# Recurrent attention over 64 segments on one core: every second step runs its projections in reverse, the last projection's streamed weights stay for the next step, nine stream slots

## The chip, the cores and the metric

One core of one Trainium2 chip runs one program. The metric is the device time in microseconds. TensorE (PE), VectorE (DVE), ScalarE (ACT), GpSimd (POOL) and SyncE (SP, which here only issues loads) work side by side and wait for one another by semaphores; 16 DMA engines move data between HBM and the on-chip memory.

## The reference

```python
# A: x (1, 2048, 1024) layer-normed, 64 segments of 32 rows; 32 heads of 128; 8 memory rows
mem = mem0
for s in range(n_seg):                       # 64 steps, each needs the last one's output
    h = concatenate([mem, xs], axis=1)       # 8 + 32 rows
    q, k, v = h @ Wq, h @ Wk, h @ Wv         # 1024 -> 4096 each
    p = softmax(where(mask, q @ k.T * scale, -1e9))
    o = (p @ v) @ Wo                         # 4096 -> 1024
    mem = o[:, :M, :]                        # the next step's memory rows
    outs.append(o[:, M:, :])
# B: the two rows with the largest x @ w_r pass through a gated MLP (1024 -> 3584 -> 1024)
# result: x + A + B
```

The four weight matrices together are 32 MB in bf16, more than fits on chip; all of them are needed in each of the 64 steps, which follow one another.

## The kernel before

The weights are cut in 64 **granules** of 128x2048 (512 KB). Granules 0 to 47 belong to Q, K and V: eight granules per half matrix (16 heads), numbered q0, k0, q1, k1, v0, v1 (0/1 is the half); 48 to 63 are the output projection, two heads each. A step goes through seven **passes** p: 0 to 5 are the six half projections in that order, 6 is the output projection of 16 granules; (p, kc) is a place in them.

Forty-four granules are resident on chip. Twenty are streamed (`STREAMED`): loaded anew in every step by SP, in the order of their use, into five rotating slots. `fetch` issues the next load as soon as `after` reports a slot's granule as used up. Two exceptions keep weights in PSUM: granule 6 (`KEPT_WHOLE`) is not loaded at all, `bring_back` copies its four pieces from PSUM; of granule 25 (`KEPT_PART`) only half is loaded and `kept_piece` copies the rest. In step 0 everything comes from the inputs; `keep` turns the kept pieces into PSUM, and `copy_block` writes each other streamed granule to a DRAM scratch `wsc`, contiguous, which all later steps load from.

Each granule is multiplied with the step's 32 rows (`ST`; 24 rows of the segment and 8 memory rows) in four matmuls of 512 columns on four column strips of PE. The last eight rows of each of the four segments of a group do not depend on the memory, so their projections are made once per group of four steps, spread as extra passes over the granules (`PASSES`, the "left-over rows", tiles `PSl`, `WL`); their Q and K go through DRAM (`ql_d`) and come back as `LX`.

What follows a projection is hung up at fixed places by `hook(p, kc, ...)`, run after that granule's matmuls: `transposes` turns q and k, `scores` multiplies them, adds the mask on DVE, takes the maximum and subtracts it, `exponent` is on ACT, `soften` normalises and transposes the probabilities to `PT` on DVE, `attend` multiplies them with V (two halves `ph` per half of the heads) and casts the sums to `OT`. Half 0's scores stand at (2, 6) and its attention at (5, 4) and (5, 6); half 1's scores at (4, 6), exponent at (5, 0), attention in the output projection ahead of its granules 5 and 8. In that projection the next segment is normalised and turned too. A step ends with the DVE addition of the output (line 842), the stores, and the turning of the new memory rows into the next `ST`.

Lines in the profile: 354 the streamed load in `fetch`, 388 `copy_block`, 365 and 370 the turnings in `keep`, 377 `bring_back`, 381 `kept_piece`, 774 the projections' matmuls (`PSm`), 567 the left-over passes, 574 `project` (`WO` for the step, `WL` for left-over rows), 624 `transposes`, 490 the turning of `LX` (fetched in 483), 647 and 649 `scores`, 656 to 662 mask, maximum and subtraction, 666 `exponent`, 671 to 682 `soften`, 696 and 698 `attend`, 705 and 707 its casts, 793 and 803 the casts of a finished projection, 842 the step's last addition. The changed kernel has its own numbers.

After the last step the MoE weights are loaded into the homes of the residents and the two routed rows are done.

```python
def fetch():
    s, g = flow.pop(0)
    t = wstream.tile([P, 2048], BF16, tag="g", name="g")
    ...
        nc.sync.dma_start(out=t[:, c], in_=wsc[g][:, :])
# (5, 6): attend(0, 1); output projection:
for w in range(16):
    if w == 5:
        attend(1, 0)
    if w == 8 and s + 1 < NSEG:
        attend(1, 1, lambda: turned.append(turn_rows(xn, left_too)))
    Gv = granule(48 + w)
    project(WO, w, Gv, lhs_main, w == 15, first=(w == 0))
```

Of the kernel before, what the change touches and what calls it, by code (L numbers as in the profile page):

```python
# [17 lines left out]
N_RES = 44  # L18
N_SLOT = 5
KEPT_WHOLE = 6  # L20
KEPT_PART = 25
NEG = -30000.0

PHASES = [(0, 0), (1, 0), (0, 1), (1, 1), (2, 0), (2, 1)]

STREAMED = [2, 5, 6, 9, 13, 17, 21, 25, 29, 33, 36, 39, 42, 45, 47, 50, 53, 56, 59, 62]

UNIT_PHASE = {"q0": 0, "k0": 1, "q1": 2, "k1": 3, "v0": 4, "v1": 5, "o": 6}
PASSES = {
# [11 lines left out]
}  # L44

COPIES = {"q0": (1, 1, 0, "scalar"), "q1": (1, 5, 7, "vector"), "k0": (2, 2, 0, "scalar"), "k1": (3, 1, 0, "scalar"),
          "v0": (3, 4, 7, "scalar"), "v1": (3, 5, 7, "scalar"), "o": (0, 4, 3, "vector")}
# [3 lines left out]
def kernel(  # L51
# [46 lines left out]
    assert len(streamed) == NG - N_RES  # L98
    n_str = len(streamed)
    resident = [g for g in range(NG) if g not in streamed]  # L100

    def granule_dram(g):
        if g < 48:
            p, kc = divmod(g, KC)
            mat, half = PHASES[p]
# [11 lines left out]
    wstream = ctx.enter_context(tc.tile_pool(name="wstream", bufs=N_SLOT))  # L117
# [24 lines left out]

    def load_resident(g):
# [11 lines left out]
    NEGR = CT[:, 13:14]  # L155
# [8 lines left out]
    PTB2 = BT[:, 256:512].bitcast(BF16)  # L164
    OPB = BT[:, 256:256 + 4 * NK]
# [110 lines left out]
    def norm_seg(s):  # L276

        x = X[s % 2]
        mr = two_rows(MR[:, s, :], "ri")
        ab = mr[:, 2:4]  # L280
        nc.vector.tensor_scalar(out=ab[:, 0:1], in0=mr[:, 1:2], scalar1=1.0, scalar2=KMSK, op0=ALU.add, op1=ALU.mult)
        nc.vector.tensor_scalar(out=ab[:, 1:2], in0=mr[:, 0:1], scalar1=mr[:, 1:2], scalar2=-1.0, op0=ALU.mult, op1=ALU.mult)
        xn = front.tile([P, 256], BF16, tag="st", name="XN")
        nc.vector.tensor_scalar(out=xn[:, :], in0=x[:, :], scalar1=mr[:, 0:1], scalar2=mr[:, 1:2],
                                op0=ALU.subtract, op1=ALU.mult)
        nc.vector.tensor_scalar(out=x[:, :], in0=x[:, :], scalar1=ab[:, 0:1], scalar2=ab[:, 1:2],
                                op0=ALU.mult, op1=ALU.add)
        return xn

    def turn(src, at=0):  # L290
        PTx = PTB[:, 256 * at:256 * (at + 1)].rearrange("p (c g r) -> p c g r", c=2, g=4)
# [8 lines left out]
    def turn_rows(xn, xl):  # L300

        return turn(xn), turn(xl, 1) if xl is not None else None

    def new_st(turned):
        PTx, PTl = turned
        st = front.tile([P, KC, SEG], BF16, tag="st", name="ST")
        nc.scalar.copy(out=gview(st)[:, :, :, 0:XM], in_=PTx[:, :, :, 0:XM])
        if PTl is None:
            return st, None
        stl = one.tile([P, KC, SEG], BF16, tag="stl", name="STL")  # L310
        nc.scalar.copy(out=gview(stl), in_=PTl[:, :, :, :])
        return st, stl
# [16 lines left out]
    def sum_left(t, G):  # L329
# [9 lines left out]
    queued = []  # L339
# [3 lines left out]
                 KEPT_PART: {2: KEPT[2][:, 0:512], 3: KEPT[2][:, 512:1024]}}  # L343

    def fetch():
        if not flow:
            return
        s, g = flow.pop(0)
        t = wstream.tile([P, 2048], BF16, tag="g", name="g")
        c = columns(g, s)  # L350
        if s == 0:
            nc.sync.dma_start(out=granule_out(t, g), in_=granule_dram(g))
        elif c is not None:
            nc.sync.dma_start(out=t[:, c], in_=wsc[g][:, :])
        queued.append((g, t))
# [4 lines left out]

    def keep(g, t):
        for c, K in KEPT_COLS[g].items():
            turned = PTB.rearrange("p (i r) -> p i r", i=4)
            for i in range(4):
                nc.tensor.transpose(out=turned[:, i, :], in_=t[:, 512 * c + P * i:512 * c + P * (i + 1)],
                                    identity=IDENT[:, :])
            XK = one.tile([P, 512], BF16, tag="vl0", name="XK")
            nc.vector.tensor_copy(out=XK[:, :], in_=PTB)
# [4 lines left out]
    back = [None] * 4  # L373

    def bring_back(c, copy):
        back[c] = one.tile([P, 512], BF16, tag=(roles[0], "bE", "kt", "bC")[c], name="BK")
        copy(out=back[c][:, :], in_=KEPT_COLS[KEPT_WHOLE][c])  # L377

    def kept_piece(g, c, copy):
        t = [t for q, t in queued if q == g][0]  # L380
        copy(out=t[:, 512 * c:512 * (c + 1)], in_=KEPT_COLS[g][c])  # L381


# [6 lines left out]
    to_copy = list(streamed)  # L390
    flow += [(s, g) for s in range(NSEG) for g in streamed if s == 0 or g != KEPT_WHOLE]

# [5 lines left out]
    def fetch_moe():  # L398
        while moe and free_homes:
            what = moe.pop(0)  # L400
            h = free_homes.pop(0)
            t = home(h, [P, 2048], BF16, "MW") if h >= 0 else wstream.tile([P, 2048], BF16, tag="g", name="g")
# [9 lines left out]
    def granule(g):  # L412
        if g in res_tiles:
            return res_tiles[g]
        got, t = queued.pop(0)
        assert got == g, (got, g)
        return t
# [11 lines left out]
    n_q = 0  # L429
    for g in range(48):  # L430
        if g in streamed:
            n_q += 1
            if n_q < N_SLOT:
                fetch()
            continue
        if n_q >= N_SLOT:
            break
        load_resident(g)
        if g % 2 == 1 and n_x < NT // 2:
            load_x(n_x)  # L440
            n_x += 1
    todo_res = [g for g in resident if g not in res_tiles]
# [4 lines left out]
    ST, STL = new_st(turn_rows(norm_seg(0), XL0))  # L447
# [11 lines left out]
    def after(s, g):  # L459

        if s == 0:
            if g in side:
                side[g]()
            if g % 2 == 1 and g >= 8 and to_copy:
                copy_block(to_copy.pop(0))
            if n_x_left and g % 2 == 1:
                load_x(n_x_left.pop(0))
            while todo_res and todo_res[0] <= g + 2 * 64 // n_str + 8 and (todo_res[0] < resident[-10] or g >= 2 * NT + 12):
                load_resident(todo_res.pop(0))
        if g in streamed and (s == 0 or g != KEPT_WHOLE):  # L470
            fetch()
        if s == NSEG - 1:
            if g in resident:
                free_homes.append(g)
            if not flow:
                fetch_moe()
# [493 lines left out]
```

## Time and profile before

| | |
|---|---|
| median of 3 runs | 1895.43 us (1892.03 to 1902.41) |
| profiled execution | 1896.06 us, of it span 1894.4 us |
| busy share | PE 83%, DVE 46%, ACT 36%, POOL 23% |
| DMA | 712.41 MB, mean 376 GB/s |
| TensorE clock granted | mean 0.960 |

"Busy" is the share of the span in which an engine had an instruction running; for PE the ends of matmuls are modelled, so busy isn't full speed. In the digits of the slices, 9 is 90% or more. In rows of waits the numbers are the total in us, how often, and the longest. In timeline rows they are start, duration, engine, line, operation, output and inputs.

### The profile page before, as it was taken

To read this page: it belongs to the slowest core of one execution; us is meant where nothing else is said; L and a number is where in the kernel's file an instruction comes from. 1 tells how busy PE (TensorE), PEld (TensorE's weight loads), DVE (VectorE), ACT (ScalarE), POOL (GpSimd) and SP (SyncE) were. 2 spreads that over 40 slices of the span, in tenths; PEclk is the share of its full clock that TensorE was granted. 3 is DMA by queue.
4 is the path that set the end of the run, shared out by engine and by line. 5 is a ranking of instruction groups with operands and counts; after the bars stand their busy time and mean duration, and the time that the engine had idled before them with its cause. 6 is when DMAs were issued, how large, how long until landed. Compare 5 with 4: busy or idle time off the path is not lost.

```text
span 1894.4 us, 82425 instructions
## 1 busy us (share of the span) xinstructions
PE 1572.3 (83%) x36000; PEld 880.0 (46%) x36000; DVE 875.6 (46%) x2865; ACT 683.5 (36%) x1916; POOL 441.5 (23%) x882
## 2 busy tenths in 40 slices
PE   3458888889888888898888988888888889888864
PEld 1124545455454444445454545445444554545443
DVE  6734544445444444544454444444444454444430
ACT  1123433344333433434333334333433343433320
POOL 3111313213131322213121322213132221312120
PEclk8669999999999999999999999999999999999985
DMA  9999999999999999999999999999999999999998
GB/s 370 398 368 379 369 386 373 391 378 390 393 360 375 368 380 372 379 372 374 401 365 374 370 388 370 355 383 374 379 364 387 377 392 378 364 395 362 374 388 331
DMA packets 232121, 712.41 MB, mean 376 GB/s; under 512 B 39296, under 2 KB 53168, under 8 KB 231760
## 3 DMA queue, kind: packets, MB, share of 16 engines
q1 hardware_dynamic: 194384, 671.18, 92.9%
q0 software_dynamic: 28736, 28.09, 4.6%
q10 hardware_dynamic: 8640, 7.87, 1.2%
q8 instruction: 282, 4.62, 0.9%
q14 instruction: 79, 0.65, 0.1%
HBM read 694.32 MB, written 22.29 MB: 378 GB/s over the span
## 4 chain that ended last, share of the span: by engine, by line
DMA 53%; PE 38%; DVE 5%; issue 2%; ACT 1%; SPq 1%; ACTq 0%; DVEq 0%
DMA g<-wsc 47%; PE PSm L774 21%; PE WO L574 4%; PE PSl L567 4%; PE BT L624 3%; PE WL L574 2%; DMA XP<-in_A_x_dram 2%; DMA MW<-in_B_w_gate_dram 1%; DVE XR L248 1%; DMA MW<-in_B_w_up_dram 1%; DMA g<-in_A_Wq_dram 1%; DMA wres<-in_A_Wo_dram 1%; PE BS L647 1%; DMA g<-in_A_Wo_dram 1%; PE BT L293 1%
## 5 line engine op out<-in xcount | busy, mean ns | idle before, releaser
L774 PE MATMUL PSm<-wres,ST 128*32 128x512 bf16 x8448 | 706.5, 383 | 9.1 <-DMA wres<-in_A_Wv_dram 3.5
L774 PEld LDWEIGHTS <-ST 128*32 128x32 bf16 x12288 | 328.6, 96 | 403.5 <-issue 176.3
L774 PE MATMUL PSm<-g,ST 128*32 128x512 bf16 x3588 | 361.9, 387 | 106.2 <-DMA g<-wsc 81.5
L574 PEld LDWEIGHTS <-OT 128*32 128x32 bf16 x8192 | 219.2, 97 | 153.3 <-issue 135.8
L793 ACT CAST XB<-PSm 128x512 bf16<-128x512 f32 x256 | 150.1, 586 | 310.8 <-PE PSm L774 309.9
L574 PE MATMUL WO<-wres,OT 128*32 128x256 bf16 x5632 | 238.3, 278 | 13.7 <-DMA wres<-in_A_Wo_dram 7.9
L483 POOL DMA_DIRECT2D LX<-ql_d x63 | 33.6, 533 | 825.9 <-PE WO L574 396.5
L574 PE MATMUL WO<-g,OT 128*32 128x256 bf16 x2560 | 132.3, 281 | 83.6 <-DMA g<-wsc 74.1
L567 PE MATMUL PSl<-wres,STL 128*32 128x512 bf16 x2112 | 192.7, 391 | 0.0
L844 POOL DMA_DIRECT2D out_dram<-X x256 | 129.4, 512 | 217.1 <-DVE X L842 168.3
L639 DVE COPY KT<-BT 128x512 bf16<-128x512 bf16 x112 | 45.7, 408 | 283.3 <-ACT XB L793 119.0
L273 POOL DMA_DIRECT2D X<-in_A_x_dram x256 | 129.7, 510 | 186.4 <-PE PSm L774 83.8
L377 ACT COPY BK<-KEPT 128x512 bf16<-128x512 bf16 x126 | 74.4, 590 | 129.3 <-PE WO L574 98.3
L632 ACT COPY QT<-BT 128x512 bf16<-128x512 bf16 x128 | 74.9, 585 | 122.2 <-PE BT L490 70.3
L567 PEld LDWEIGHTS <-STL 128*32 128x32 bf16 x3072 | 83.6, 98 | 54.0 <-issue 8.4
L624 PEld LDWEIGHTS <-XB 128*128 128x128 bf16 x1024 | 58.5, 98 | 107.6 <-ACT XB L793 66.4
L842 DVE TENSOR_TENSOR X<-WO,X 128x256 bf16<-128x256 f32 x64 | 27.2, 424 | 170.9 <-PE WO L574 170.9
L803 ACT CAST VM<-PSm 128x512 bf16<-128x512 f32 x128 | 75.6, 591 | 81.2 <-PE PSm L774 79.6
L696 PEld LDWEIGHTS <-VM 32*128 32x128 bf16 x2048 | 66.1, 91 | 82.9 <-issue 69.9
L624 PE MATMUL BT<-IDENT,XB 128*128 128x128 bf16 x1024 | 102.0, 222 | 1.4 <-ACT QKL L502 1.4
L381 DVE COPY g<-KEPT 128x512 bf16<-128x512 bf16 x126 | 47.6, 419 | 118.2 <-PE PSm L774 74.4
L705 DVE CAST OT<-BT 128x128 bf16<-128x128 f32 x128 | 37.3, 291 | 129.8 <-PE BT L293 68.8
(168 smaller groups left out, 2378.9 us busy)
## 6 DMA issues: line engine op xcount, KB each, us to landing
g<-wsc SPq DMA_DIRECT2D x1134, 512.0 KB, 6.1
g<-wsc SPq DMA_DIRECT2D x63, 256.0 KB, 5.4
LX<-ql_d POOLq DMA_DIRECT2D x63, 128.0 KB, 5.9
ql_d<-XBl ACTq DMA_DIRECT2D x60, 128.0 KB, 5.6
MW<-in_B_w_gate_dram SPq DMA_DIRECT2D x16, 448.0 KB, 9.1
MW<-in_B_w_up_dram SPq DMA_DIRECT2D x16, 448.0 KB, 9.1
wres<-in_A_Wk_dram SPq DMA_DIRECT2D x12, 512.0 KB, 11.5
MW<-in_B_w_down_dram SPq DMA_DIRECT2D x12, 512.0 KB, 10.1
```

The source lines that it names most:

```text
L273: nc.gpsimd.dma_start(out=X[s % 2][32 * g:32 * g + XM, :], in_=x2[s * SEG:s * SEG + XM, 256 * g:256 * (g + 1)])
L377: copy(out=back[c][:, :], in_=KEPT_COLS[KEPT_WHOLE][c])
L381: copy(out=t[:, 512 * c:512 * (c + 1)], in_=KEPT_COLS[g][c])
L567: nc.tensor.matmul(PSl[32 * jq:32 * jq + 32, :], lhsT=STL[:, g % KC, :], rhs=part(Gv, jq), start=first_, stop=last_, tile_position=(0, 32 ...
L574: nc.tensor.matmul(PS[32 * g:32 * g + 32, 0:256], lhsT=lhs(h), rhs=Gv[:, D * hs + 256 * g:D * hs + 256 * (g + 1)], start=(first and hs == ...
L624: nc.tensor.transpose(out=PTq[:, il, :, :].rearrange("p j r -> p (j r)"), in_=XB[:, il * P:(il + 1) * P], identity=IDENT[:, :])
L632: nc.scalar.copy(out=QT[half][:, :, :], in_=pv)
L696: nc.tensor.matmul(o, lhsT=VM[half][q0:q0 + 32, il * P:(il + 1) * P], rhs=PTm[q0:q0 + 32, il, 0:NK], start=True, stop=False, tile_position ...
L774: nc.tensor.matmul(PSm[32 * jq:32 * jq + 32, :], lhsT=ST[:, kc, :], rhs=part(Gv, jq), start=(kc == 0), stop=(kc == KC - 1), tile_position= ...
L793: nc.scalar.copy(out=XB[:, :], in_=PSm[:, :])
L803: nc.scalar.copy(out=VM[half][:, :], in_=PSm[:, :])
L844: nc.gpsimd.dma_start(out=out2[s * SEG:s * SEG + XM, 256 * g:256 * (g + 1)], in_=OB[32 * g:32 * g + XM, :])
```

## The change

- Even steps run v0, q0, k0, q1, k1, v1; odd steps v1, q1, k1, q0, k0, v0 (`ORDER`; `a` is the half that comes first, `b` the other). So the pass before the output projection and the next step's first pass use the same eight granules. Five of them are streamed, and they are not loaded for the next step: they stay in their slots (`held_over`) until its first pass has used them. Within the output projection odd steps begin with granules 56 to 62.
- Nine slots in place of five; 39 residents and three quarters of granule 12 (`PIECED`) in place of 44; the fourth quarter of 12 is kept in PSUM. Streamed: 24. `KEPT_WHOLE` is now granule 63, the last of the step; `bring_back` copies it at places 9 and 11 of the output projection.
- Scores, exponent and attention have new places: half a's scores at (3, 6), attention at (5, 3) and (5, 6); half b's scores at (5, 5), exponent and `soften` at (5, 6) behind the second attention of a, attention in the output projection ahead of place 7 (even) or 6 (odd), and 9.
- The mask is put into the scores' PSUM by three PE matmuls with the identity ahead of the scores; DVE no longer adds it. `norm_seg` is split, and part of it stands earlier. `LX` is fetched behind place 15 of the output projection, before behind 9, and turned in pass 2, before in pass 1. Some copies change between ACT and DVE. `PASSES` and `COPIES` are new throughout (one entry shown).

```diff
-N_RES = 44
-N_SLOT = 5
-KEPT_WHOLE = 6
+N_SLOT = 9
+KEPT_WHOLE = 63
 KEPT_PART = 25
+PIECED = 12
-STREAMED = [2, 5, 6, 9, 13, 17, 21, 25, 29, 33, 36, 39, 42, 45, 47, 50, 53, 56, 59, 62]
+STREAMED = [1, 5, 9, 13, 17, 21, 25, 27, 30, 35, 36, 37, 38, 39, 43, 44, 45, 46, 47, 50, 53, 58, 61, 63]
+V_FIRST, V_LAST = [3, 4, 5, 6, 0, 1, 7, 2], [3, 0, 1, 4, 5, 6, 7, 2]
+O_ORDER = [list(range(48, 64)), [*range(56, 63), *range(48, 56), 63]]
+def order_of(odd):
+    a, b = odd, 1 - odd
+    out = [[32 + 8 * a + c for c in V_FIRST]]
+    out += [[16 * half + 8 * mat + c for c in range(8)] for half in (a, b) for mat in range(2)]
+    return out + [[32 + 8 * b + c for c in V_LAST], O_ORDER[odd]]
-    "v1": {(3, 5, 2): [42], (3, 5, 3): [40, 41], (3, 5, 4): [43], ...
+    "v1": {(2, 6, 5): [40], (2, 6, 6): [41], (2, 7, 0): [42, 43], ...
...
+    def held_over(s, g):
+        return s + 1 < NSEG and g in ORDER[s % 2][5] and g in streamed
+    def loaded(s, g):
+        return g in streamed and (s == 0 or not (g == KEPT_WHOLE or g in ORDER[s % 2][0]))
...
     def fetch():
-        s, g = flow.pop(0)
-        t = wstream.tile([P, 2048], BF16, tag="g", name="g")
+        while flow and slots:
+            s, g = flow.pop(0)
+            slot = slots.pop(0)
+            t = wres.tile([P, 2048], BF16, tag=slot, name="g")
...
-        if g in streamed and (s == 0 or g != KEPT_WHOLE):
+        if g in queued and not held_over(s, g):
+            slots.append(queued.pop(g)[0])
             fetch()
...
+            if mat == 1:
+                for S4, m in ((SPS[:, :, 0, 0:XM], MASK), (SPS[:, :, 0, SEG:NK], NEGR.to_broadcast([P, XL])),
+                              (SPS[:, :, 1, SEG:NK], MASK[:, 0:XL])):
+                    nc.tensor.matmul(S4, lhsT=IDENT[:, :], rhs=m.unsqueeze(1).to_broadcast([P, 4, S4.shape[2]]),
+                                     start=(m is MASK), stop=False, skip_group_check=True)
...
-        hook(2, 6, lambda: scores(0))
-        hook(3, 4, exponent)
-        hook(3, 4, lambda: soften(0))
+        hook(3, 6, lambda: scores(a))
+        hook(4, 1, exponent)
+        hook(4, 1, lambda: soften(a))
...
-        hook(4, 6, lambda: scores(1))
-        hook(5, 0, exponent)
-        hook(5, 0, lambda: soften(1))
-        hook(5, 4, lambda: attend(0, 0))
-        hook(5, 6, lambda: attend(0, 1))
+        hook(5, 3, lambda: attend(a, 0))
+        hook(5, 5, lambda: scores(b))
+        hook(5, 6, lambda: attend(a, 1))
+        hook(5, 6, exponent)
+        hook(5, 6, lambda: soften(b))
...
+        for n, g in enumerate(order[6]):
+            if n == 7 - a:
+                attend(b, 0)
+            if n == 9 and s + 1 < NSEG:
+                attend(b, 1, lambda: turned.append(turn(xn, BS[:, 160:288].bitcast(BF16))))
...
+            if s > 0 and n in (9, 11):
+                c = n // 2 - 4
+                bring_back(c, a, nc.vector.tensor_copy)
+                bring_back(2 + c, a, nc.scalar.copy)
```

More of the change, by code (lines that the diff above doesn't have):

```diff
@@ L412, in granule @@
     def granule(g):
[L413 to L417, printed above, removed]
+        if g == PIECED:
+            return list(pieced)
+        if g == KEPT_WHOLE and g not in queued:
+            return back
+        return res_tiles[g] if g in res_tiles else queued[g][1]
     load_x(0)
@@ L446 @@
     norm_left(XL0, 0)
-    ST, STL = new_st(turn_rows(norm_seg(0), XL0))
+    MR0 = norm_rows(0)
+    ST = new_st(turn(norm_seg(0, MR0), PTS[:, 0:256]))
+    sum_seg(0, MR0)
+    STL = new_stl(turn(XL0))
     mem_to_st(OB, ST)
@@ L473, in after @@
             if g in resident:
-                free_homes.append(g)
+                free_homes.append(f"wres{g}")
             if not flow:
+                free_homes.extend(slots)
+                slots.clear()
                 fetch_moe()
@@ L770 @@
             for kc in range(KC):
-                g = 8 * p + kc
-                Gv = back if s > 0 and g == KEPT_WHOLE else granule(g)
+                g = order[p][kc]
+                Gv = granule(g)
                 for jq in range(4):
-                    nc.tensor.matmul(PSm[32 * jq:32 * jq + 32, :], lhsT=ST[:, kc, :], rhs=part(Gv, jq),
+                    nc.tensor.matmul(PSm[32 * jq:32 * jq + 32, :], lhsT=ST[:, g % KC, :], rhs=part(Gv, jq),
                                      start=(kc == 0), stop=(kc == KC - 1), tile_position=(0, 32 * jq))
```

329 lines of the change are left out of this document (181 added, 148 removed), and 22 rows, old and new, of the table PASSES.

## The prediction

> **What bounds the kernel now.** I read the page first, then the DMA queues over the steady part, then the steps and waits there, then single timelines. A "step" is one of the 64 segments; a "granule" is one 128x2048 piece of weight (512 KB); "position" is a granule's place in its step, 0 to 63, with 48 to 63 the output projection; even and odd are the step's number.
>
> ```profile
> span 1894.4 us, 82425 instructions
> PE 1572.3 (83%) x36000; PEld 880.0 (46%) x36000; DVE 875.6 (46%) x2865; ACT 683.5 (36%) x1916; POOL 441.5 (23%) x882
> DMA  9999999999999999999999999999999999999998
> DMA 53%; PE 38%; DVE 5%; issue 2%; ACT 1%; SPq 1%; ACTq 0%; DVEq 0%
> ```
>
> PE is busy 83% of the time and the DMA line never leaves its top digit, so the question is which of the two gives the other its pace. The chain that ended last is more DMA than PE. The next rows are the DMA queues from 130 to 1838 us, the busy times of the same stretch, and the one DVE addition (line 842) that closes each of the 64 steps.
>
> ```profile
> DMA packets 206514, 642.51 MB, mean 376 GB/s; under 512 B 36191, under 2 KB 49871, under 8 KB 206171
> q1 hardware_dynamic: 172795, 612.27, 94.1%
> 130.00:1838.00 1708.00, 1496.98 (x34690) 838.11 (x34689) 791.82 (x2645) 661.35 (x1866) 406.38 (x805) 0.99 1.00 376
> L842 DVE TENSOR_TENSOR X<-WO,X x64: 423/425/426, 129.4 to 1837.7; 128x256 bf16<-128x256 f32 x64
> ```
>
> Sixty-three steps lie between 129.4 and 1837.7: **27.12 us a step**. DMA share is 1.00 over all of it: the 16 engines have no free time left, at 376 GB/s. Queue q1, which carries the streamed weights, holds 94.1% of it, 0.941 x 1708 / 63 = 25.51 us a step. A step streams 18 whole granules and one half (1134 and 63 issues over 63 steps on the page), 18.5 in all, so **one granule costs 1.38 us** of DMA time. The page's rows of those issues, the waits of PE in the same stretch, and three granules of one projection as PE takes them:
>
> ```profile
> g<-wsc SPq DMA_DIRECT2D x1134, 512.0 KB, 6.1
> g<-wsc SPq DMA_DIRECT2D x63, 256.0 KB, 5.4
> ...
> PE PSm L774 <- DMA g<-wsc: 81.5, 173, 1.7
> PE WO L574 <- DMA g<-wsc: 74.1, 161, 1.9
> PE WO L696 <- ACT OTL L707: 11.5, 15, 2.1
> ...
> 919.36 0.39 PE L567 MATMUL PSl<-wres,STL 128*32 128x512 bf16 x4
> 919.58 0.39 PE L774 MATMUL PSm<-wres,ST 128*32 128x512 bf16 x4
> 919.79 0.39 PE L774 MATMUL PSm<-g,ST 128*32 128x512 bf16 x4
> ```
>
> 155.6 us, or 2.47 a step, is waiting for streamed weights, in 334 waits; the next kind is 11.5 us. So without DMA waits PE would need at most 27.12 - 2.47 = 24.65 us a step. It may need less: four matmuls are drawn 0.39 us long but follow the last four after 0.22, so each wait can hide some 0.17 us behind matmuls still drawn, 334 x 0.17 / 63 = 0.9 us a step, which gives 23.75 as the lower end.
>
> **The change part by part: traffic.** On SP, between an output projection and the first projections behind it, before (the number after wsc is the granule, the one behind it the buffer):
>
> ```order
> L354 DMA g_21274<-wsc62_123 128x2048
> L354 DMA g_21321<-wsc2_105 128x2048
> L354 DMA g_21375<-wsc5_106 128x2048
> L354 DMA g_21407<-wsc9_107 128x2048
> L354 DMA g_21433<-wsc13_108 128x2048
> ```
>
> and now, from an even step into an odd one:
>
> ```order
> L387 DMA g_22637<-wsc61_124 128x2048
> L387 DMA g_22807<-wsc17_106 128x2048
> L387 DMA g_22841<-wsc21_107 128x2048
> L387 DMA g_22937<-wsc25_108 128x1024
> L387 DMA g_22969<-wsc27_109 128x2048
> L387 DMA g_23018<-wsc30_110 128x2048
> ```
>
> Before, the next step's first projection is fetched from its first streamed granule on. Now the five streamed granules of that projection (43 to 47 here) have no row: they are still in their slots. A step loads 24 - 1 - 5 = 18 granules, one a half: 17.5 against 18.5. That is one granule, 1.38 us: if DMA stays without a gap, the step falls to **25.74 us**, 1.47 for each granule left, the other queues' share in it.
>
> **Where a gap can come.** Five of nine slots are shut through the output projection, so only four turn over. The end of one projection before, and the landings of all streamed loads:
>
> ```profile
> 907.63 0.19 PE L696 MATMUL BS<-PT,VM 32*128 32x40 bf16 x1
> ...
> 908.09 0.40 PE L574 MATMUL WO<-g,OT 128*32 128x256 bf16 x8
> 910.62 0.40 PE L574 MATMUL WO<-g,OT 128*32 128x256 bf16 x8 [0.24 <-DMA g<-wsc]
> 912.02 0.40 PE L574 MATMUL WO<-g,OT 128*32 128x256 bf16 x8 [0.56 <-DMA g<-wsc]
> 912.23 0.40 PE L574 MATMUL WO<-wres,OT 128*32 128x256 bf16 x8
> ...
> 913.82 0.61 PE L774 MATMUL PSm<-wres,ST 128*32 128x512 bf16 x8
> DMA to landing us min/median/max: 3.5/6.1/10.6
> ```
>
> From the granule 53 (908.09) to the next step's first matmul is 5.73 us, less 0.80 of DMA waits, 4.9; with the other attention half (907.63 to 908.09, 0.46) and one granule, 0.22, PE needs 5.6 us from 53's landing until it gives back the first shut slot. In that stretch DMA has 58 and 61 to bring, and the loads into the four slots as they turn over: six granules x 1.47 = 8.8 us from an odd step into an even one, 5.5 x 1.47 = 8.1 from an even one, where one of the four (25) is a half. A load needs time ahead of its first byte: of the quickest landing, 3.5 us, 1.38 is transfer, and I put half of the other 2.1 ahead of it, 1.1. So DMA stays fed while PE's stretch is under 7.7 or 7.0 us.
>
> Three waits are added to the 5.6. First, the projections of a half begin one granule behind its attention: its cast (0.27, seen below) less a granule, plus start-up, 0.3. Second, granule 63 comes back from PSUM in four copies at the end of the projection, of which ACT makes two behind its casts:
>
> ```profile
> L377 DVE COPY BK<-KEPT x126: 411/415/425, 119.3 to 1807.8; 128x512 bf16<-128x512 bf16 x126
> L377 ACT COPY BK<-KEPT x126: 585/589/606, 120.3 to 1806.8; 128x512 bf16<-128x512 bf16 x126
> LX<-ql_d POOLq DMA_DIRECT2D x63, 128.0 KB, 5.9
> ```
>
> Attention to last copy on ACT is two casts, ST and two copies of 0.59, near 2.0 us; PE reaches 63 after six granules, some 1.4: 0.6. Both were off PE's path before. (The last row: LX is now fetched behind position 63 instead of 57, and turned by PE in the third pass, after the step's end of 1.4 and twenty granules or 4.4 us and its passes. With 5.9 to landing that is a wait of 0 to 0.4, but five fresh loads are in flight there, so DMA doesn't feel it.) Third, the softmax. On ACT, at the second half's exponent, before (the exponent ahead of the first half's attention casts):
>
> ```order
> L803 CAST VM<-PSm 128x512
> L666 ACTIVATE BS<-BS 128x320
> L705 CAST OT<-WO 128x128
> L707 CAST OTL<-WO 128x4x8
> L705 CAST OT<-BT 128x128
> L707 CAST OTL<-BT 128x4x8
> ```
>
> and now:
>
> ```order
> L772 CAST OT<-WO 128x128
> L774 CAST OTL<-WO 128x4x8
> L772 CAST OT<-BT 128x128
> L774 CAST OTL<-BT 128x4x8
> L728 ACTIVATE BS<-BS 128x320
> L878 CAST VM<-PSm 128x512
> ```
>
> The exponent now queues behind four casts, and its scores have moved from the sixth granule of the pass before last to the fifth of the last. Its chain, from the trace of before:
>
> ```profile
> 928.54 0.49 DVE L661 TENSOR_REDUCE NM<-BS 128x8 f32<-128x320 f32 x1
> 929.06 0.50 DVE L662 TENSOR_TENSOR BS<-BS,NM 128x320 f32<-128x320 f32 x1
> 929.59 0.42 ACT L666 ACTIVATE BS<-BS 128x320 f32<-128x320 f32 x1 [1.07 <-DVE BS L662]
> 931.75 0.45 DVE L682 STREAM_TRANSPOSE PT<-OTL 128x256 bf16<-128x256 bf16 x1
> 930.37 0.27 ACT L705 CAST OT<-WO 128x128 bf16<-128x128 f32 x1 [0.35 <-PE BT L698]
> 930.76 0.22 ACT L707 CAST OTL<-BT 128x32 bf16<-128x32 f32 x1
> ```
>
> Exponent to last transpose is 932.20 - 929.59 = 2.61 us; the exponent starts after one granule (0.22), an attention half (0.46), 0.2 and four casts (930.37 to 930.98, 0.61), so the operand is ready 4.1 us after the scores. PE meanwhile has nine granules (1.9), that attention and some two passes of left-over rows (0.4), 2.8: a bare wait of up to 1.3 us. Queued behind it on PE are granules 55 on, and so on SP the loads into the slots of 58 and 61; behind the exponent on ACT stands the cast of VM, which the same attention needs. Where PE waits there for 47, 50 and 53 anyway, the softmax is done by then and the wait is nought. The stretch so becomes 6.5 to 7.8 us against 7.7 and 7.0, a DMA gap of 0 to 0.1 in one kind of step and 0 to 0.8 in the other, mean 0 to 0.45. I take 0.35, near the upper end, since casts and start-ups were counted without any slip. **A step: 25.74 + 0.35 = 26.09 us.** Edits at nothing: the first half's softmax (thirteen positions, two turnings and the last pass's 0.2 for a chain of 932.20 - 928.54 + 0.2 = 3.9), the mask put in by three PE matmuls of 160 columns in place of three DVE operations (at most one granule's 0.22 per half, under DMA cover; bare, it lengthens the stretch), granule 12's fourth piece (one DVE copy of 0.42 under the exponent).
>
> **Start and end.** Before 130 us everything is DMA too. The software queue in that window, and PE turning two pieces of the kept granule:
>
> ```profile
> q0 software_dynamic: 3616, 10.62, 21.2%
> 27.78 0.62 PE L365 MATMUL BT<-IDENT,g 128*128 128x128 bf16 x4
> 29.32 0.63 PE L365 MATMUL BT<-IDENT,g 128*128 128x128 bf16 x4
> ```
>
> Of the first 130 us, 21.2% or 27.6 went to the software queue, nearly all of it 18.5 granule copies into the scratch; 22.5 now, four more at up to 1.49: +6.0. Turning the kept granule into PSUM takes 1.54 us a piece; for granule 6 that stood early in step 0, for 63 it stands at its very end: four pieces, with ACT's slower copy 1.7 each, 6.9 us, and the 1.6 of a step's end (912.23 to 913.82), while only 2.5 loads (3.5 us) are open. Between 0 and 8.5 of DMA gap; I take 5.0. The MoE tail moves the same bytes: 0.
>
> **The sum**, against the profiled execution's own 1896.06 (span 1894.4, the median of the runs is 1895.43, 0.6 below): 1896.1 - 63 x (27.12 - 26.09) + 11 = 1896.1 - 64.9 + 11 = **1842 us**.
>
> **The rivals.** (a) DMA has no gap at all: PE's DMA waits cover each new one, as the 1.00 of now suggests. 1896.1 - 63 x 1.38 + 6 = 1815 us. Against it speak the two narrow margins above. (b) PE becomes the bound: 23.75 plus 0.3, 0.6 and 1.3 is 26.0; 24.65 plus these, 0.4 of masks and 0.4 for LX is 27.65; middle 26.8, so 1896.1 - 20 + 11 = 1887. For it: nothing of 2.47 us covers a softmax that starts late in every step. Against: these waits fall where PE waits for DMA now.
> (c) Slower: DMA runs dry once a step, at the turn of the step, and each refill is paid in full. A load into an empty queue takes the 3.5 us of the quickest landing, 2.1 more than its share: 25.74 + 2.1 = 27.84, so 1896.1 + 45 + 11 = 1952. It decides from a mean gap of 27.12 - 25.74 - 11/63 = 1.2 us on, that is when PE's stretch passes about 8.6 us instead of 6.5 to 7.8. For it: four live slots instead of five; against: the median landing of 6.1 us says that four to five loads are in flight, and four are left.
> The Trainium skill, DMA: Bandwidth & Descriptors, section Anatomy of one DMA, speaks for (c): each DMA has a fixed cost near 2.0 us besides bytes at 436 GB/s (told of the software path), 3.2 us for 512 KB alone, and by it a step of (c) is an estimated 27.7 us, 1947 in all. This trace agrees with its size (3.5 at the least) and shows that with four in flight it is not paid: 1.38.
> That the loads aren't saved is excluded by the rows of SP.
>
> **How the numbers follow.** Forecast (steps of 25.85 to 26.5, 1827 to 1868 us): 0.52. (a) 0.15. (b) 0.20 (1868 to 1906). (c) 0.13. About 0.5%, 9.5 us, is what a measurement of this kernel can tell from no change, so the borders are 1886 and 1905: of (b) 0.12 is faster and 0.08 the same. Faster 0.52 + 0.15 + 0.12 = 0.79, same 0.08, slower 0.13. The range goes from just under (a), 1812, to where (b) nearly ends, 1900, and leaves out (c) and a little of (b).
>
> **What would show it.** Right: 17.5 granules a step on q1, 33 MB less; steps near 26.1 between the additions that close them; DMA share 0.98 to 0.99; PE's waits for streamed weights smaller than 155 us, and new ones for PT (softmax) and BK at the end of the projection. (a) shows 1.00 and 25.7. (b) shows a DMA share under 0.97 and PE waits for ACT and DVE above 60 us. (c) shows landings near 3.5 us and DMA waits grown. The step of the sum most open is the 0.35; wrong altogether would be a granule that no longer costs 1.38.

## The result, and the profile after

The changed kernel takes **1987.38 us** (median of 4 runs, 1986.39 to 1990.35) against 1898.92 for the kernel before on the same chip: 1.0449 times as long, 95% interval 1.0406 to 1.0492. The forecast was 1842, the range 1812 to 1900. It is slower, and outside the range.

Four lines of the changed kernel's page:

```profile
span 1985.6 us, 82542 instructions
PE 1667.1 (84%) x36392; PEld 932.2 (47%) x36392; DVE 807.8 (41%) x2698; ACT 682.2 (34%) x1857; POOL 449.7 (23%) x902
DMA  9989899899998899999899999899999999899998
DMA packets 223767, 681.48 MB, mean 343 GB/s; under 512 B 38368, under 2 KB 52368, under 8 KB 223408
```

The traffic fell by 30.9 MB (33 forecast). But the DMA line now has eights in it, and over the whole execution the rate is 343 GB/s in place of 376. Next come the addition that closes each step, the steady part between the first and the last of these (the last columns are granted clock, DMA share, GB/s), its stream queue, the issues of the streamed loads and PE's waits for them:

```profile
L925 DVE TENSOR_TENSOR X<-WO,X x64: 424/425/427, 143.0 to 1928.5; 128x256 bf16<-128x256 f32 x64
143.00:1928.50 1785.50, 1587.99 (x35100) 891.51 (x35100) 728.07 (x2488) 659.89 (x1808) 412.98 (x822) 0.95 0.93 342
q1 hardware_dynamic: 163851, 579.85, 87.1%
g<-wsc SPq DMA_DIRECT2D x1071, 512.0 KB, 9.0
PE PSm L848 <- DMA g<-wsc: 121.8, 204, 1.6
PE WO L636 <- DMA g<-wsc: 1.9, 5, 0.7
```

A step takes (1928.5 - 143.0) / 63 = **28.34 us**, 1.22 more than before; over the 63 steps that is 77.2 us. The first step ends 13.6 us later (143.0 against 129.4). Together that is 90.8 of the 91.2 us between the profiled executions (1987.29 and 1896.06).

Two things changed. The DMA share of the steady part is 0.93, where before it was 1.00. And PE's waits for streamed weights, before split evenly between the half projections (81.5 us) and the output projection (74.1), are now all in the half projections: in the output projection there is next to none. There the weights come early, and behind them DMA falls off. The next two lines are DMA's busy tenths in 40 slices of the same 20.4 us of a step, from the start of the last half projection to well into the next step, first before, then after:

```profile
DMA  9999999999999999999999999999999999799999
```

```profile
DMA  9999999999999996495899977668899954999998
```

In the changed kernel, SP issues a single load in the first 7.7 us of that stretch (first and last start):

```profile
L387 SPq DMA_DIRECT2D g<-wsc x1: 319/319/319, 1018.0 to 1018.0; - x1
```

That load is granule 53. It landed at 1028.0, and PE reached it at 1030.0. From 1018.0 to 1025.8 no slot came free: five held the next step's first granules, and the other four held or awaited granules of the output projection, of which PE needs only four in sixteen places. In the trace, the loads in flight (issued and not landed) when PE begins five positions of the step, the last being the first of the next step, mean over 52 steps, are:

| position | 43 | 48 | 53 | 58 | next step's 0 |
|---|---|---|---|---|---|
| before | 4.0 | 3.7 | 3.8 | 3.9 | 4.1 |
| changed | 6.9 | 3.5 | 3.0 | 1.6 | 2.0 |

What that does to the rate can be read in the same trace. The same 52 steps of the changed kernel, cut into slices of half a microsecond and sorted by the loads in flight:

| loads in flight | 1 | 2 | 3 | 4 | 5 | 6 | 7 | 8 |
|---|---|---|---|---|---|---|---|---|
| share of the time | 2% | 14% | 17% | 9% | 9% | 11% | 24% | 14% |
| GB/s, all traffic | 183 | 273 | 284 | 362 | 364 | 375 | 384 | 392 |

A third of the time there are three or fewer in flight, and DMA then moves under 290 GB/s. In the kernel before that is 8% of the time; it has four or five in flight otherwise, at 374 and 391 GB/s. The many loads in flight earlier in the step don't make up for it, since the rate rises little beyond four.

### The profile page after: what moved, and what is told of

It reads as the page before. It is cut to its first block, busy times and chain, and to the rows that moved or that the text cites. A ratio compares the mean times of both kernels' runs of the same rounds, so it can differ in the third digit from the quotient of the medians.

```text
span 1985.6 us, 82542 instructions
## 1 busy us (share of the span) xinstructions
PE 1667.1 (84%) x36392; PEld 932.2 (47%) x36392; DVE 807.8 (41%) x2698; ACT 682.2 (34%) x1857; POOL 449.7 (23%) x902
## 5 line engine op out<-in xcount | busy, mean ns | idle before, releaser
L848 PE MATMUL PSm<-wres,ST 128*32 128x512 bf16 x7168 | 588.1, 388 | 11.3 <-DMA wres<-in_A_Wq_dram 7.2
L848 PE MATMUL PSm<-g,ST 128*32 128x512 bf16 x4864 | 458.0, 390 | 128.6 <-DMA g<-wsc 121.8
L636 PE MATMUL WO<-wres,OT 128*32 128x256 bf16 x5632 | 278.3, 309 | 11.5 <-DMA wres<-in_A_Wo_dram 3.8
L636 PEld LDWEIGHTS <-OT 128*32 128x32 bf16 x8192 | 234.1, 107 | 108.3 <-issue 60.7
L708 DVE COPY KT<-BT 128x512 bf16<-128x512 bf16 x64 | 27.1, 423 | 373.5 <-issue 227.3
L629 PE MATMUL PSl<-g,STL 128*32 128x512 bf16 x1216 | 121.5, 388 | 0.0
L772 DVE CAST OT<-BT 128x128 bf16<-128x128 f32 x192 | 56.0, 292 | 151.7 <-PE BT L765 150.2
L772 ACT CAST OT<-WO 128x128 bf16<-128x128 f32 x128 | 34.1, 266 | 242.6 <-PE BT L765 242.6
L723 DVE TENSOR_REDUCE NM<-BS 128x8 f32<-128x320 f32 x128 | 63.0, 492 | 122.0 <-PE BS L718 122.0
L772 ACT CAST OT<-BS 128x128 bf16<-128x128 f32 x128 | 34.1, 266 | 205.4 <-PE BT L765 134.0
```

The source lines that it names most:

```text
L629: nc.tensor.matmul(PSl[32 * jq:32 * jq + 32, :], lhsT=STL[:, g % KC, :], rhs=part(Gv, jq), start=first_, stop=last_, tile_position=(0, 32 ...
L636: nc.tensor.matmul(PS[32 * g:32 * g + 32, 0:256], lhsT=lhs(h), rhs=quarter(Gv, 4 * hs + g), start=(first and hs == 0), stop=(last and hs = ...
L723: nc.vector.tensor_reduce(out=NM[:, :], in_=S8, axis=AX.X, op=ALU.max, negate=True)
L772: copy(out=OT[half][ph][:, jl, :, :], in_=ov[:, :, 0:SEG])
L848: nc.tensor.matmul(PSm[32 * jq:32 * jq + 32, :], lhsT=ST[:, g % KC, :], rhs=part(Gv, jq), start=(kc == 0), stop=(kc == KC - 1), tile_posit ...
```

## The experiments

Sixteen kernels were run. The steps in the table are read as above, from the first closing addition to the last; those in the expectations are means over 52 steps in the middle, 0.05 to 0.2 us less. "Us a load" is the step divided by its loads, idle time and other traffic included. "Live" is the number of slots that turn over at the turn of the step. Ratios are to the kernel before on the same chip (median 1904 to 1908 us there, 1899 for the row "changed").

| kernel | loads | live | us | ratio (95%) | step | DMA share | us a load |
|---|---|---|---|---|---|---|---|
| before | 18.5 | 5 | | | 27.12 | 1.00 | 1.47 |
| changed | 17.5 | 4 | 1987.4 | 1.045 (1.041 to 1.049) | 28.34 | 0.93 | 1.62 |
| b_small | 18.5 quarters | 5 | 1688.0 | one run | 23.83 | 0.44 | |
| small | 17.5 quarters | 4 | 1763.5 | one run | 24.90 | 0.40 | |
| expfirst | 17.5 | 4 | 1985.0 | 1.042 (1.033 to 1.050) | 28.22 | 0.94 | 1.61 |
| warm | 17.5 | 4 | 1977.7 | 1.036 (1.031 to 1.042) | 28.26 | 0.94 | 1.61 |
| b_slot3 | 18.5 | 3 | 2452.0 | one run | 35.84 | 0.86 | 1.94 |
| b_slot4 | 18.5 | 4 | 2097.5 | 1.101 (1.097 to 1.104) | 30.17 | 0.95 | 1.63 |
| b_slot6 | 19.5 | 6 | 1905.4 | 0.999 (0.996 to 1.001) | 27.08 | 1.02 | 1.39 |
| hold4 | 18.5 | 5 | 1996.2 | 1.047 (1.043 to 1.050) | 28.62 | 0.96 | 1.55 |
| oorder | 17.5 | 4 | 2049.9 | 1.076 (1.073 to 1.079) | 29.35 | 0.91 | 1.68 |
| spread | 17.5 | 4 | 1953.6 | 1.025 (1.019 to 1.032) | 27.67 | 0.96 | 1.58 |
| b_bunch | 18.5 | 5 | 1998.4 | 1.048 (1.041 to 1.054) | 28.84 | 0.96 | 1.56 |
| hold4s | 18.5 | 5 | 1953.2 | 1.025 (1.022 to 1.028) | 27.89 | 0.98 | 1.51 |
| hold4s_early | 18.5 | 5 | 1914.6 | 1.007 (1.002 to 1.011) | 27.09 | 1.00 | 1.46 |
| spread_early | 17.5 | 4 | 1926.4 | 1.011 (1.009 to 1.013) | 27.44 | 0.96 | 1.57 |
| slot8_early | 17.5 | 4 | 1933.8 | 1.016 (1.010 to 1.022) | 27.45 | 0.97 | 1.57 |
| hold4s_early_warm | 18.5 | 5 | 1962.7 | 1.030 (1.023 to 1.037) | 27.92 | 0.98 | 1.51 |

**Is PE, or one of the added waits, the bound?** `small` and `b_small` load only the first 512 columns of each streamed granule and multiply with these four times over; `expfirst` swaps two hooks; `warm` keeps PE running.

```diff
# small, b_small (the load alone; PE's reading of it four times is left out)
-                nc.sync.dma_start(out=t[:, c], in_=wsc[g][:, :])
+                nc.sync.dma_start(out=t[:, 0:512], in_=wsc[g][:, 0:512])
# expfirst
+        hook(5, 6, exponent)
         hook(5, 6, lambda: attend(a, 1))
-        hook(5, 6, exponent)
         hook(5, 6, lambda: soften(b))
# warm: behind the matmuls of granule kc of a projection
+                for _ in range({3: 1, 4: 3, 5: 2}.get(kc, 0) if p == 5 and s > 0 else 0):
+                    for jq in range(4):
+                        nc.tensor.matmul(PSm[32 * jq:32 * jq + 32, :], lhsT=ZW[:, :], ...  # zeros
```

Expected of b_small: 

> The same cut in the kernel before. Its PE alone by the prediction: 23.75 to 24.65 us a step, 1685 to 1740 us; theory A says nothing else.

Expected of small: 

> The changed kernel with each streamed load after step 0 cut to its first 512 columns, which PE reads four times over (the results are other ones; PE's work and order are the same). It shows PE's own pace. Theory A: PE alone needs 24.5 to 25.5 us a step, 1745 to 1805 us. Rival P (PE's path sets the step): above 1900.

Expected of expfirst: 

> The changed kernel with the second half's exponent and its softmax issued ahead of the first half's second attention, so that on ACT the exponent no longer stands behind the casts of that attention. If the late softmax cost what the prediction allowed for it at the most (0 to 1.3 us a step), a step falls by up to 0.6 us and the time to about 1950. If, as the waits of the changed kernel say (under 5 us in all for the softmax), it costs nothing: 1980 to 1992.

Expected of warm: 

> The changed kernel with six sets of four extra matmuls (zero weights, so nothing is added) in the last pass before the output projection, at the granules where PE waits for one load after another; they fill its waiting time. If the half clock that follows that waiting (3.0 us a step) lengthens the output projection and so the time DMA is short of loads: half clock under 1.5 us a step, 1935 to 1965 us. If the clock drops are without effect, since PE is ahead of DMA over the whole step: 1980 to 2000.

Without the loads' time the changed kernel would step in 24.90 us, 3.4 below what it takes, so PE and all waits among the engines are not the bound. The change costs PE 24.90 - 23.83 = 1.07 us a step. With the exponent ahead of the attention's casts (its `soften` stays behind them) the step is 28.22 against 28.34, so the late exponent isn't the cause. The added matmuls raise the granted clock from 0.95 to 0.99 and take 0.1 us from the step. So the lower clock is a companion of the loss and not its cause.

**Does a granule have a fixed price?** `b_slot3`, `b_slot4` and `b_slot6` are the kernel before with other numbers of slots, the sixth slot paid for with one more streamed granule (15).

```diff
-N_SLOT = 5
+N_SLOT = 4        # b_slot4; 3 in b_slot3; 6 in b_slot6, with N_RES = 43 and 15 in STREAMED
```

Expected of b_slot4: 

> The kernel before with four stream slots in place of five, nothing else. Theory A, with some 3 us from issue to landing beside a transfer of 1.3: three in flight are just too few where PE holds one, 1910 to 1990 us, DMA share 0.93 to 0.99. Rival P says nothing of slots: 1895 to 1905.

Expected of b_slot3: 

> The kernel before with three stream slots. Theory A: about two in flight, landings 1.9 to 2.3 us apart (as at the turn of the changed kernel's step), 18.5 x 2.1 = 39 us a step, 2500 to 2800 us. Rival P: below 2000.

Expected of b_slot6: 

> The kernel before with six slots and one resident fewer (granule 15 is streamed too): 19.5 loads a step instead of 18.5. Theory A as the last runs sharpened it (the time per load hangs on how many are in flight: 1.94 us at three slots, 1.63 at four, 1.46 at five): about 1.40 us a load at six, 27.3 us a step, 1895 to 1930 us, the load more almost paid for. The prediction's own step (a granule costs a fixed 1.38): 63 x 1.38 more, 1970 to 1995.

The steady part of b_slot4, of before (shown with the prediction, 1.00 and 376) and of b_slot6:

```profile
129.80:2030.70 1900.90, 1542.19 (x34690) 859.29 (x34690) 797.88 (x2645) 662.93 (x1866) 406.10 (x805) 0.97 0.95 337
```

```profile
132.40:1838.60 1706.20, 1510.71 (x34690) 840.81 (x34690) 791.38 (x2645) 659.50 (x1866) 406.62 (x805) 1.00 1.02 396
```

It has no fixed price. The step divided by its loads is 1.94, 1.63, 1.47 and 1.39 us with three, four, five and six slots; the loads in flight are then 2.6, 3.5, 4.3 and 5.1 in the mean. (In the prediction's measure, q1's busy share alone, a load takes 1.58, 1.46, 1.38 and 1.33 us: it moves less, since it leaves out other traffic and the time in which DMA isn't busy.) Four slots cost more than was expected, three a little less. Six slots bring 19.5 granules in the time of 18.5: at "share 1.00" there were still 20 GB/s to be had, and the share went on to 1.02.

**Is it the number of live slots alone, or when the granules are asked for?** `hold4` loads one held granule (39 or 47) again, which leaves five slots live. `oorder` takes the streamed granules of each half of the output projection sooner, so that their slots come back sooner. `spread` makes 13 and 27 resident and streams 48 and 56: six streamed granules in the output projection instead of four; with that, one left-over pass (granule 54) moves from the first step of a group to the last, in `hold4s` below too. `b_bunch` is the kernel before with 43 and 44 streamed in place of 56 and 59, as unevenly as the changed kernel, and with nothing held.

```diff
# hold4: AGAIN = (39, 47) isn't held (the matching edit of loaded() is left out)
-        return s + 1 < NSEG and g in ORDER[s % 2][5] and g in streamed
+        return s + 1 < NSEG and g in ORDER[s % 2][5] and g in streamed and g not in AGAIN
# oorder
-O_ORDER = [list(range(48, 64)), [*range(56, 63), *range(48, 56), 63]]
+O_ORDER = [[50, 53, 48, 49, 51, 52, 54, 55, 58, 56, 57, 61, 59, 60, 62, 63], [58, 61, 56, ...]]
# spread (PASSES left out)
-STREAMED = [1, 5, 9, 13, 17, 21, 25, 27, 30, 35, 36, 37, 38, 39, 43, 44, 45, 46, 47, 50, 53, 58, 61, 63]
+STREAMED = [1, 5, 9, 17, 21, 25, 30, 35, 36, 37, 38, 39, 43, 44, 45, 46, 47, 48, 50, 53, 56, 58, 61, 63]
# b_bunch, on before
-STREAMED = [2, 5, 6, 9, 13, 17, 21, 25, 29, 33, 36, 39, 42, 45, 47, 50, 53, 56, 59, 62]
+STREAMED = [2, 5, 6, 9, 13, 17, 21, 25, 29, 33, 36, 39, 42, 43, 44, 45, 47, 50, 53, 62]
```

Expected of hold4: 

> Four granules stay for the next step in place of five; 39 or 47 is loaded again, so a step loads 18.5 granules, as before the change, and five slots turn over at the step's end. Theory A (at the turn of the step the live slots are full of landed granules that PE has not reached yet; fewer than three loads are in flight, and DMA idles about 2 us a step): at least three in flight at the turn, DMA share 0.97 or more, steps near 27.3 us, 1905 to 1945 us in all, that is faster than the changed kernel although it loads 31.5 MB more. Rival P (PE's longer path at the end of the step, with its clock drops, sets the step; DMA idles only because it is ahead): a granule more can only cost, 1987 or up to 1.38 x 63 = 87 us more.

Expected of oorder: 

> The output projection takes its streamed granules first within each half of the heads (50, 53 at places 0, 1 and 58, 61 at 8, 11 in even steps; 58, 61 at 0, 1 and 50, 53 at 7, 11 in odd ones, before 2, 5, 10, 13 and 2, 5, 9, 12), so their slots are given back earlier; loads and work are the same. Theory A: DMA idles 0.3 to 0.6 us a step less, 1950 to 1968 us. Rival P: 1980 to 1995, or slower if PE now waits for 50 and 58 at the start of the projection.

Expected of spread: 

> The changed kernel with the same 17.5 loads a step, nine slots and five held granules, but with other granules streamed: 13 and 27 become resident, 48 and 56 are streamed instead, so the output projection asks for six streamed granules instead of four, and the stretch between the last projection and the next step's second pass is less empty. Theory (demand for streamed granules is uneven over the step: landed granules sit in the four live slots while PE works through residents, and the loads in flight fall to about two): more loads are asked for at the turn of the step, loads in flight there rise from 1.6 to 2.2 towards 3, a step takes 27.3 to 27.9 us instead of 28.3, 1925 to 1960 us. Rival (four live slots alone set the pace, wherever demand lies): 28.2 to 28.4 a step, 1980 to 1995. By a fixed price of a granule (the prediction): no change either, 17.5 loads as before, 1987.

Expected of b_bunch: 

> The kernel before with its five slots, 18.5 loads and nothing held, but with granules 43 and 44 streamed in place of 56 and 59: five streamed granules in the last half projection and three in the output projection, as unevenly as in the changed kernel. Theory (uneven demand alone costs time, since slots then hold landed granules that PE does not need yet): 27.6 to 28.5 us a step instead of 27.04, 1935 to 1990 us. Rival (it is the holding of five granules, with slots shut, and not the places of the streamed granules): 27.0 to 27.2, 1900 to 1915. By a fixed price of 1.38 us for a granule: no change, 1906.

The first theory, that the fourth live slot is too few, fell with hold4: the fifth live slot was worth no more than the added load cost. oorder fell too: PE now waits 54.6 us for weights in the output projection. Its slots come back sooner, but their next granules are needed some twenty places later: the first two of each step land 6.5 and 5.6 us ahead of PE on the mean (5.1 and 4.4 in the changed kernel), and so their slots stand full. Loads in flight at position 58 fell from 1.6 to 1.4. The second theory, uneven demand, holds in both directions. spread, with the same loads, slots and holding, takes 0.67 us off a step; it has 2.6 loads in flight at position 58 instead of 1.6. The gain lies in the two middle steps of a group (28.0 and 27.7 us to 26.4 and 26.6), which the moved left-over pass doesn't touch. b_bunch, with the slots and loads of before, costs 1.72 a step, more than was expected; its waits for streamed weights are:

```profile
PE PSm L774 <- DMA g<-wsc: 192.5, 302, 2.3
PE WO L574 <- DMA g<-wsc: 5.2, 10, 1.7
```

This is much the picture of the changed kernel: waits bunched in the half projections, none in the output projection, a DMA share of 0.96. (b_bunch's granted clock was 0.92; how much of its 1.72 us the clock makes was not separated.)

**Both together, and what stands behind them.** `hold4s` holds four granules (39 and 47 become resident, 48 and 56 streamed), which gives five live slots and an evened demand.

Expected of hold4s: 

> The changed kernel with four granules held through the turn of the step instead of five, and an evened demand: 39 and 47 become resident, 48 and 56 are streamed instead. So the last projection asks for four streamed granules instead of five, the output projection for six instead of four, five of nine slots live at the turn, and a step loads 18.5 granules, as before the change. Theory (time for a load follows the loads in flight, and those follow live slots and even demand): four to five in flight at the turn as in the kernel before, more elsewhere, so 18.5 loads at 1.41 to 1.47 us, 26.1 to 27.2 us a step, with the later start (13 us) 1850 to 1920 us. Rival (holding granules costs by itself, as four held with the uneven demand took 28.53 a step): 27.9 to 28.6 a step, 1960 to 2000 us. By a fixed price of 1.38 us: 27.1 a step, 1905 to 1915.

At 27.89 it missed. But its mean hides two kinds of steps. Within a group of four, from one step's first projection to the next one's, the two middle steps take 26.4 us each, inside the forecast of this run; the last takes 28.7 and the first 29.6. Two rows of its waits show what the first step pays:

```profile
ACT STL L342 <- DMA out_dram<-OL: 49.4, 14, 3.9
PE PSl L629 <- ACT STL L342: 30.7, 14, 2.8
```

ScalarE copies the next group's left-over rows (`STL`) into a buffer from which the last group's output (`OL`) must first be stored, once a group of four, and PE waits 2.2 us behind it. In the changed kernel itself that second row is 7.6 us in 6 times. The `early` kernels make the left-over output projection's last passes and its store about eight positions sooner; `slot8_early` has one slot less and 27 resident.

```diff
# hold4s_early and spread_early, on hold4s and spread
-          (3, 8, 0): [51, 52], (0, 1, 4): [55], (0, 2, 3): [59], (0, 3, 3): [60], (0, 4, 2): [62]},
+          (3, 8, 0): [51, 52], (0, 0, 3): [55], (0, 1, 4): [59], (0, 2, 3): [60], (0, 3, 3): [62]},
-          ... "o": (0, 4, 3, "vector")}
+          ... "o": (0, 3, 4, "vector")}
# slot8_early, on hold4s_early (27 also leaves STREAMED)
-N_SLOT = 9
+N_SLOT = 8
```

Expected of hold4s_early: 

> The kernel with four held granules and the evened demand, and the left-over rows' last additions and their store moved about eight positions earlier in the first step of each group (four of the output projection's left-over passes earlier, the copy at the fourth pass instead of the fifth), so that the store is done before the next left-over rows are copied into the same buffer. If that wait is what the first step of a group pays (2.9 + 1.2 us at two positions where others take 1.1 + 0.5): that step falls from 29.7 by 1.5 to 2.5 us, the mean from 27.79 to 27.2 to 27.5, 1920 to 1940 us. If the loads pay it anyway: less than 0.2 us a step, 1945 to 1960 us.

Expected of spread_early: 

> The kernel with five held granules and the evened demand, with the same earlier store. If the wait for the store is what the first step of a group pays (2.2 + 1.1 us where others take 1.3 + 0.6): that step falls from 28.5 by 1 to 1.5 us, the mean from 27.59 to 27.2 to 27.4, 1930 to 1945 us. If the loads pay it anyway: less than 0.2 us a step, 1945 to 1960 us.

Expected of slot8_early: 

> The kernel with four held granules, evened demand and the earlier store, with eight slots instead of nine: granule 27 becomes resident, so a step loads 17.5 granules as in the changed kernel, and four slots are live at the turn. If evened demand makes the saved load worth its price even with four live slots: 25.9 to 26.6 us a step, 1850 to 1890 us. If four live slots at the turn cost what the load saves (three in flight there, as in the evened kernel with five held): 26.8 to 27.3, 1905 to 1935 us.

Expected of hold4s_early_warm: 

> The same with nine slots and 18.5 loads, and zero-weight matmuls at three places of the last half projection that keep TensorE running through its waits. If the lower granted clock (0.9 us a step at half) still costs: 26.7 to 26.85 us a step, 1900 to 1910 us. If loads alone set the pace: no change, 1908 to 1920; if the added matmuls delay TensorE, slower than 1920.

PE's wait for the store is gone, and hold4s falls by 0.80 us a step, more than expected; spread falls by 0.23, as expected. The steady part of hold4s_early and its waits:

```profile
145.60:1852.10 1706.50, 1533.09 (x35100) 861.72 (x35100) 724.43 (x2489) 661.96 (x1808) 412.65 (x822) 0.98 1.00 377
PE PSm L848 <- DMA g<-wsc: 36.3, 64, 1.7
PE WO L636 <- DMA g<-wsc: 32.2, 76, 0.9
```

That is the kernel before again: 18.5 loads, share 1.00, 377 GB/s, waits split evenly, and a step of 27.09 against 27.12. Holding granules, then, needn't cost anything in the step. What keeps this kernel 0.7% slower is its start, 16.2 us later (145.6 against 129.4). slot8_early shows what the saved load is worth: with four live slots, 17.5 loads take 27.45 us, and so they do in spread_early. A load is saved (1.46 us) and the others become 0.105 dearer (17.5 x 0.105 = 1.83): a loss of 0.4 us a step. The added matmuls, put into hold4s_early, cost 0.83 a step, the outcome that its expectation named last: PE has no slack of that size there. No kernel tried is measurably faster than the one before.

## Why the prediction was wrong

**The step that failed** is "Where a gap can come": its mean gap of 0.35 us, in whose place DMA stood idle for some 1.98 us a step. It let PE's stretch begin at the landing of granule 53, as before the change, where PE stands waiting for it (74.1 us of waits in the output projection). With nine slots and only four streamed granules in sixteen places, those granules come early; PE reaches 53 after it has landed (waits there 1.9 us). The four live slots are then not being filled while PE works, they stand full. And it took DMA as fed as long as any load is open; with two or three in flight the trace has 273 and 284 GB/s, with four 362. The row that should have warned was in the change itself: five streamed granules in the last half projection, then four in sixteen, then none in eight.

**The size of it.** By its share of 0.93, DMA is busy for 26.36 of the 28.34 us and idle for 1.98. The forecast had 25.74 of DMA work and 0.35 idle. So idle time makes 1.63 us of the miss, and more DMA time the other 0.62. This is an account by shares and rough: where loads follow each other without a gap the share reads 1.03. The price of a granule hardly moved: in the prediction's own measure, q1's share, it is 0.871 x 1785.5 / 63 / 17.5 = 1.41 us against 1.38. The gap is the term that was mis-sized, and the prediction had called the 0.35 its most open step. Its other warning, a granule that no longer costs 1.38, came true in another sense: a transfer saved is worth 1.38 only if DMA stays as full as it was, and "DMA share is 1.00: the 16 engines have no free time left" was a misreading, since b_slot6 moved 20 GB/s more.

**The rivals.** (c), that DMA runs dry at the turn of the step, was right in sign, place and kind, and had a chance of 0.13. Its point of decision, a mean gap of 1.2 us, was passed (1.98). Its price of one refill, 27.84 a step, was 0.5 short. The estimate of 27.7 that went with it from the Trainium skill, DMA: Bandwidth & Descriptors, section Anatomy of one DMA, was 0.6 short (and 27.7 us a step sum to some 1945, not 1947). Nor did its sign come as written: the loads that SP issues next in the stretch above, from 1025.8 to 1030.6, land after 3.6 to 5.3 us, but the median landing rose from 6.1 to 9.0 us, since six to eight loads are in flight in the passes before. (a) is out with the share of 0.93. (b) is out with the 24.90 of small, under its lowest 26.0; of its signs the share under 0.97 came, but PE's waits for ACT and DVE are some 38 us and not above 60.

**What held.** 17.5 loads a step, and 31 MB less (the 33 forecast left out the four granules more that are copied to the scratch). PE's lower end without DMA waits, 23.75: b_small measured 23.83. The start: 13.6 us later against 11. The added waits came near the lower ends: PE waits 2.6 us in all for the softmax's `PT`, 6.7 for LX, and the waits show none for the returned granule. The added work of PE is 1.07 us a step, half of the 2.2 that (b) added at the least, and it lies under DMA.

**Not foreseen.** Waits that bunch in the last half projection lower PE's clock (below), and `STL` waits for the store of `OL`, which costs time as soon as the loads cost less. What makes the last step of a group slow in the evened kernels (28.4 us in hold4s_early against 25.9 to 26.8 for the other three) stays open; small has no such step (24.9 against 24.5 to 25.0).

## What to carry to other kernels

A DMA share of 1.00 does not fix a price per transfer; measure the price with a slot more and a slot less before counting what a saved transfer brings. A buffer that keeps data for later is taken from prefetch exactly while it keeps: here, with demand evened, a slot at the turn of the step was worth more than the load that it replaced (27.09 against 27.45 us a step). And streamed pieces want to be spread as PE needs them in time: look for the longest stretch of resident work and ask how many loads the open slots can take in it.

## What the runs showed of the hardware

The rate of DMA goes with the loads of 512 KB in flight. Over whole steps, with three to six slots: 284 GB/s at 2.6 in flight, 337 at 3.5, 376 at 4.3, 396 at 5.1. Within the changed kernel: 273 GB/s at two, 362 at four, 392 at eight (the table above). A load that is issued and has not landed doesn't keep DMA busy all that time: with one in flight the rate is 183.

TensorE's granted clock fell to half after runs of waits that were mostly under 1 us each. Three stretches of one step of the changed kernel; in the last columns the clock, the DMA share and GB/s:

```profile
993.00:996.40 3.40, 2.13 (x80) 1.22 (x80) 1.38 (x4) 0.60 (x3) 0.00 (x0) 0.97 1.03 408
996.40:999.80 3.40, 3.40 (x64) 2.46 (x64) 2.23 (x7) 1.93 (x7) 0.00 (x0) 0.53 0.57 204
999.80:1003.20 3.40, 3.38 (x118) 2.37 (x113) 1.80 (x9) 1.60 (x7) 0.00 (x0) 1.00 0.90 323
```

In the first, DMA runs full and PE takes one granule for each landing; in the second, PE has its weights but half its clock, and DMA has little left to load. Thirty-four such drops, 25 of them 3.4 us long, stand in 52 steps of the changed kernel, four in those of before. The Trainium skill, TensorE: Matmul & The Clock Gate, section HAM oscillation, ties the drop to a DMA wait longer than a window of 3.4 us; the length of the drop agrees (3.41), the wait does not: in the 6.8 us ahead of 32 of the 34 drops no gap between matmuls (by their modelled ends) is above 1.2 us, and the gaps in the last 3.4 us add up to 1.1 to 2.3 us. The other two have gaps of 2.6 and 3.6 us.
